# Scale and bias of the first feed-forward's activation: applied to the activation itself instead of behind the second matrix

## The chip, the core and the metric

The kernel runs on one core of one Trainium2 chip. The metric is the device time of one execution in microseconds (us). PE is TensorE (PEld its weight loads), DVE VectorE, ACT ScalarE, POOL GpSimd, and SP the engine that issues most DMAs. The core has on-chip memory (SBUF) and eight accumulator banks of 128 x 512 floats each (PSUM), into which PE writes.

## The reference: what is computed

Attention with a memory term over 4 batches, 8 heads, 576 positions and 64 features gives 2304 tokens of 512 values. Two feed-forwards follow:

```python
# first feed-forward: w_in 512 x 2048, w_out 2048 x 512, s and b one number each
h = x @ w_in
r = np.maximum(h, 0.0)
g = s * (r * r) + b
x = (g @ w_out).astype(np.float32)
# second feed-forward, same sizes
h = x @ w_in
P = a[0] + a[1] * h + a[2] * h2 + a[3] * h3        # h2 = h*h, h3 = h2*h
Q = 1.0 + np.abs(b[0]) * np.abs(h) + np.abs(b[1]) * h2
g = P / (Q + 1e-06)
return (g @ w_out).astype(np.float32)
```

Since s and b are single numbers, g @ w_out equals s * ((r * r) @ w_out) + b * (column sums of w_out). The kernel before uses the right-hand form; the changed kernel uses the left-hand one.

## The kernel before

The four weight matrices come as float64, the rest as float32. Each matrix product is taken as three products of a split pair (a high part in the reduced float32r format, and the rest), so an activation is always handed to PE as two tiles, high and low: `gh` and `gl`.

The program has these stages. Attention runs in 32 units (16 pairs of heads, low and high half of the positions), their tiles named q, k, vm, s (scores), p, pt/th (transposed probabilities), pf/fs (the memory term's input), av and xp (the output). While it runs, the weights of the first half of the first feed-forward are decoded from float64 (`decode`: one ACT and some five DVE or POOL instructions on 128 x 512; tiles dAi, dAo for the resident half, dB for the half that is stored to DRAM as `w1d`). Block A, nine pieces of 256 tokens, computes the first 1024 hidden features and stores a partial sum `x2p`; seven of the nine pieces are interleaved with attention. Block B, five pieces of 512, 512, 512, 384 and 384 tokens, does the other 1024 features, adds `x2p`, and stores `x2T`; meanwhile the second feed-forward's matrices are decoded (d2i, d2o). Block C, the same five pieces, is the second feed-forward.

In blocks A and B a step `up` multiplies by w_in into a bank `ha` or `hb`, `relu_square` (line 914) makes `gh` and `gl` of it, and a step `down` multiplies these by w_out. `interleave` puts up(f+1) between up(f) and down(f). `relu_square` before is: ACT relu to a tile `r`, ACT square of `r` to `gh`, DVE max(h,0)*r written back into the bank, DVE bank minus `gh` to `gl`. The square and the product need nothing of each other.

Scale and bias come behind block B (line 1027): one ACT instruction per output tile, with `sc1` as scale and the column `bcs` as bias. `bcs` is made from `wsum`, the sum over all decoded w_out tiles, which `decode` builds with one addition per w_out tile (`total`, line 430: 16 additions), and which four small matmuls with a vector of ones reduce (`colsum`, line 1251). The four parameter loads stand in `params` (line 1187), on SP's queue.

The order of instructions is not the code's order. `op` records each operation with the engines that may take it (`ways`, with an estimated cost), what it reads and writes, and a due time; `Plan.run` then simulates the five engines with these estimates, hands each operation to an engine, and emits it. Every engine then works through its list in order. An operation that disappears, or takes longer to become ready, thus moves others on all engines. POOL cannot read PSUM. PSUM banks are handed out in the same simulation and are free again when the last reader is done: the bank of `ha` or `hb` is held until `gl` is made.

Of the kernel before, what the change touches and what calls it, by code (L numbers as in the profile page):

```python
# [20 lines left out]
P = 128  # L21
# [4 lines left out]
def f32(ap):  # L26
    return ap.bitcast(F32)
# [221 lines left out]
def tile_kernel(ctx, tc, qk, vm, z, beta, w1i, w1o, s1, b1, w2i, w2o, a2, b2, out):  # L249
# [59 lines left out]
    nc.vector.tensor_tensor(both, ident[:, 0:64], ident[:, 64:128], ALU.add)  # L309
    wsum = cst.tile([P, DM], F32, name="wsum")  # L310
    nc.gpsimd.memset(wsum, 0.0)
    prm = cst.tile([P, 8], F32, name="prm")
    sc1, bi1 = prm[:, 0:1], prm[:, 1:2]
    a0, a1, a2_, a3 = (prm[:, 2 + i:3 + i] for i in range(4))
# [5 lines left out]
    nc.vector.memset(ones, 1.0)  # L320
    bcs = cst.tile([P, KC], F32, name="bcs")
    gate = cst.tile([P, H], F32, name="gate")
# [4 lines left out]
    omg = cst.tile([P, H], F32, name="omg")  # L327
    cst.tile([P, 40], F32, name="fill_c")
    buf("gate", None, obj=gate)
    buf("omg", None, obj=omg)  # L330
    buf("prm", None, obj=prm)
    buf("wsum", None, obj=wsum)
    buf("bcs", None, obj=bcs)
    for n in ("rec0", "rec1", "qd0", "qd1", "wsum"):
        plan.bufs[n].const = True
# [70 lines left out]

    def decode(src, nm, hi, lo, key, total=False):

# [31 lines left out]
    def w1_store(q, m, i):  # L440

        nm = f"{q}_{m}_{i}"
        parts = f"sh{nm}", f"sl{nm}"
        for n in parts:
            at_ring(n, n[:2], 2, [P, 512], F32R)
        decode(w1_source(1, q, m, i), f"dB{nm}", lambda: g(parts[0]), lambda: g(parts[1]), parts, m == 1)
        for x, n in enumerate(parts):
            load(lambda x=x: w1d[q, m, x, i], lambda n=n: f32(g(n)), P * 4 * 512, (n,), (("w1d", (q, m, x, i)),))
# [12 lines left out]
    def w1_half(k, pool):  # L461
# [12 lines left out]
        for q in range(HF // 4):  # L474
            for c in range(KC):
                sl = slice(q * 512, (q + 1) * 512)
                src = w1_source(k, q, 0, c)
                units.append(lambda c=c, q=q, sl=sl, src=src: decode(
                    src, f"d{nm}i{c}_{q}", lambda: inp("h", c, sl), lambda: inp("l", c, sl),
                    ((f"w1ih{nm}", (c, q)), (f"w1il{nm}", (c, q)))))  # L480
            for f in range(4 * q, 4 * q + 4):
                src = w1_source(k, q, 1, f % 4)
                units.append(lambda f=f, src=src: decode(
                    src, f"d{nm}o{f}", lambda: outp("h", f), lambda: outp("l", f),
                    ((f"w1oh{nm}", f), (f"w1ol{nm}", f)), True))
        return inp, outp, units
# [431 lines left out]
    def relu_square(HS, hs, w, nm):  # L918
# [9 lines left out]
        op(ways(w, -0.04), relu, (HS,), (R,))  # L928
        op(ways(w, 0.0), lambda e: e.activation(g(GH), g(R), AF.Square), (R,), (GH,))
        op(ways(w, None, 1.0), lambda e: e.scalar_tensor_tensor(hs(), hs(), 0.0, g(R), ALU.max, ALU.mult), (HS, R), (HS,))  # L930
        op(ways(w, None, 1.0), lambda e: e.tensor_tensor(g(GL), hs(), f32(g(GH)), ALU.subtract), (HS, GH), (GL,))
        return GH, GL
# [60 lines left out]
    def block_b(t0, w, at0, at1, inp, outp):  # L993
# [13 lines left out]
        def down(f):  # L1007
            GH, GL = parts[f]
            for c in range(KC):
# [11 lines left out]
                if f == HF - 1:  # L1021
# [171 lines left out]
    op(ways(1, 0.0), lambda e: e.activation(b1abs, prm[:, 7:8], AF.Abs), ("prm",), ("prm",))
# [68 lines left out]
    events.append((bB[0] - LOADS - 0.005, prior(bB[0] + 12.0, colsum)))
    for i, (t, w) in enumerate(wide):
# [85 lines left out]
```

## Time and profile before

| | us |
|---|---|
| median of 3 runs | 1061.24 |
| lowest, highest | 1059.4, 1061.42 |
| the profiled execution | 1060.15 |
| its span, first to last instruction | 1058.4 |
| PE busy in the span | 1016.3 (96%) |
| PEld, DVE | 868.7 (82%), 849.0 (80%) |
| ACT, POOL | 687.5 (65%), 414.9 (39%) |

The profiled execution lies between the lowest run and the median; 1.75 us of it lie outside the span. Busy shares are averages over the stages: attention with block A until about 406 us, the rest of block A to 456, block B to 660, block C to the end. A "wait" is idle time of an engine put down to what ended it; names after "<-" are what the instruction reads, or who released it. Buffer numbers are left out of the names, so `gla` stands for any `gl` of block A.

### The profile page before, as it was taken

The numbers are of one execution on the slowest core, as the hardware profiler recorded it, in microseconds if no ns is written. First come the engines' busy times: TensorE is split into PE (matmuls) and PEld (weight loads), VectorE is DVE, ScalarE is ACT, GpSimd is POOL, SyncE is SP. The second block draws the span as 40 slices with busy tenths as digits, with TensorE's granted clock in tenths as the row PEclk, the third lists the DMA queues.
The fourth block names the chain that finished last, engine by engine and source line by source line (L and its number), as shares of the span: only waits on it lengthen the run. The fifth ranks groups of instructions, "written<-read, shape, count | busy, mean of one in ns | idle before, by whom it ended". The sixth has DMA issues, their size and how long they took to land.

```text
span 1058.4 us, 17508 instructions
## 1 busy us (share of the span) xinstructions
PE 1016.3 (96%) x5980; PEld 868.7 (82%) x5980; DVE 849.0 (80%) x1511; ACT 687.5 (65%) x1449; POOL 414.9 (39%) x470
## 2 busy tenths in 40 slices
PE   5886999999999999999999999999999999999998
PEld 3565888878888789987778999888888888898997
DVE  5999987888779885479999543888888888887896
ACT  5866666676557653355554443877866877777895
POOL 2423221032002211012021002877777876876785
PEclk8998999999999999999999999999999999999999
DMA  6666566666656655986765332900200200010000
GB/s 196 203 191 189 150 194 207 170 201 192 192 158 187 181 176 174 365 254 206 254 204 194 102 99 65 325 1 1 78 1 0 70 1 1 23 41 1 30 1 31
DMA packets 88633, 140.42 MB, mean 133 GB/s; under 512 B 12408, under 2 KB 50400, under 8 KB 88544
## 3 DMA queue, kind: packets, MB, share of 16 engines
q1 hardware_dynamic: 83856, 130.52, 39.0%
q0 software_dynamic: 4224, 8.39, 2.5%
q8 instruction: 47, 0.77, 0.3%
q10 hardware_dynamic: 464, 0.40, 0.1%
q14 instruction: 42, 0.34, 0.1%
HBM read 103.56 MB, written 35.71 MB: 132 GB/s over the span
## 4 chain that ended last, share of the span: by engine, by line
PE 71%; DVE 13%; DMA 8%; ACT 3%; issue 2%; SPq 2%; POOL 0%; ACTq 0%; DVEq 0%; POOLq 0%
PE hc L913 19%; PE ac L1104 19%; PE ab L1017 7%; PE hb L913 7%; PE ha L913 6%; PE acc L978 6%; SPq L362 2%; PE av L857 2%; PE pt L525 2%; PE s L648 1%; DVE s L655 1%; DMA cb<-crow 1%; PE av L865 1%; DMA dAi_0r<-in_w1i 1%; PE su L682 1%
## 5 line engine op out<-in xcount | busy, mean ns | idle before, releaser
L1083 DVE RECIPROCAL qe<-qe 128x512 f32<-128x512 f32 (+2 forms) x82 | 242.6, 2959 | 49.4 <-POOL qe L378 49.4
L913 PE MATMUL hc<-xc_h,w2ih 128*128 128x512 f32 (+1 forms) x320 | 117.8, 368 | 0.0
L913 PE MATMUL hc<-xc_h,w2il 128*128 128x512 f32 (+1 forms) x320 | 117.8, 368 | 0.0
L913 PE MATMUL hc<-xc_l,w2ih 128*128 128x512 f32 (+1 forms) x320 | 117.7, 368 | 0.0
L378 POOL TENSOR_TENSOR qe<-qe,qb 128x512 f32<-128x512 f32 (+2 forms) x82 | 94.9, 1158 | 55.1 <-ACT qb L1068 54.2
L1104 PE MATMUL ac<-w2oh,ghc 128*128 128x512 f32 x288 | 112.6, 391 | 0.0
L1104 PE MATMUL ac<-w2ol,ghc 128*128 128x512 f32 x288 | 112.5, 391 | 0.0
L1104 PE MATMUL ac<-w2oh,glc 128*128 128x512 f32 x288 | 112.3, 390 | 0.0
L378 POOL TENSOR_TENSOR glc<-po,ghc 128x512 fp32r<-128x512 f32 (+2 forms) x82 | 95.0, 1158 | 23.2 <-ACT ghc L368 23.1
L378 POOL TENSOR_TENSOR pm<-pm,s 128x512 f32<-128x512 f32 (+2 forms) x82 | 95.3, 1162 | 17.1 <-ACT pm L1068 16.2
L525 PE MATMUL pt<-ident,p 128*128 128x128 f32 x320 | 62.0, 291 | 24.0 <-DVE xp L868 6.8
L1074 ACT ACTIVATE s<-hc 128x512 f32<-128x512 f32 (+2 forms) x82 | 44.6, 544 | 61.2 <-PE hc L913 58.3
L978 PE MATMUL acc<-gha,w1olA 128*128 128x256 f32 x288 | 83.7, 291 | 0.0
L978 PE MATMUL acc<-gla,w1ohA 128*128 128x256 f32 x288 | 81.5, 283 | 0.1
L978 PE MATMUL acc<-gha,w1ohA 128*128 128x256 f32 x288 | 81.3, 282 | 0.0
L666 ACT ACTIVATE p<-s,st 128x128 f32<-128x128 f32 (+3 forms) x128 | 66.5, 526 | 21.7 <-DVE st L655 20.4
L1068 ACT ACTIVATE pm<-hc,prm 128x512 f32<-128x512 f32 (+2 forms) x82 | 59.6, 726 | 22.4 <-DVE hc L1085 21.9
L525 PEld LDWEIGHTS pt<-ident,p 128*128 128x128 f32 x320 | 40.8, 147 | 38.9 <-ACT th L368 8.6
L913 PEld LDWEIGHTS hc<-xc_h,w2il 128*128 128x128 f32 x320 | 60.1, 188 | 9.1 <-DVE po L1087 0.4
L913 PEld LDWEIGHTS hc<-xc_l,w2ih 128*128 128x128 f32 x320 | 60.1, 188 | 8.6
L913 PEld LDWEIGHTS hc<-xc_h,w2ih 128*128 128x128 f32 x320 | 60.0, 188 | 7.4
L1068 ACT ACTIVATE qb<-s,cq,b1abs 128x512 f32<-128x512 f32 (+2 forms) x82 | 62.7, 764 | 2.1 <-POOL qe L378 2.1
(493 smaller groups left out, 2979.8 us busy)
## 6 DMA issues: line engine op xcount, KB each, us to landing
vm<-in_vm SPq DMA_DIRECT2D x16, 384.0 KB
k<-in_qk SPq DMA_DIRECT2D x32, 144.0 KB
x2p<-ev SPq DMA_DIRECT2D x18, 256.0 KB
out_y<-ob SPq DMA_DIRECT2D x18, 256.0 KB
qm<-in_vm SPq DMA_DIRECT2D x16, 256.0 KB
w1d<-sh SPq DMA_DIRECT2D x16, 256.0 KB
w1d<-sl SPq DMA_DIRECT2D x16, 256.0 KB
w2d<-sh SPq DMA_DIRECT2D x16, 256.0 KB
```

What stands on the lines that cost most here:

```text
L362: op({"SP": 0.1 + size / 350e3}, lambda e: e.dma_start(dst(), src()), r, w)
L378: op(ways(c, None, dve, pool), lambda e: e.tensor_tensor(dst(), x(), y(), alu), r, w, port=True)
L525: nc.tensor.transpose(dst[:, o:o + P], src, ident)
L666: e.activation(g(f"p{n}_{i}")[:, o:o + kb - ka], g(b)[:, o2:o2 + kb - ka], AF.Exp, scale=-1.0, bias=g(f"st{n}")[:, z_:z_ + 1], accum_out=g ...
L857: nc.tensor.matmul(g(AV)[64 * j:64 * j + 64, ra:rb], g(VS)[:, kb, j], g(TH)[:, o:o + rb - ra], start=x in firsts, stop=False, skip_group_c ...
L913: nc.tensor.matmul(hs(), m, y, start=c == 0 and k == 0, stop=c == KC - 1 and k == 2)
L978: nc.tensor.matmul(a, outp(y, f)[:, cs], g(z_)[:, us], start=f == 0 and k == 0 and c % 2 == 0, stop=f == HF - 1 and k == 2, skip_group_che ...
L1017: nc.tensor.matmul(g(ACC)[:, 0:w], outp(y, f)[:, cs], g(z_), start=f == 0 and k == 0, stop=f == HF - 1 and k == 2)
L1068: return lambda e: e.activation(g(dst)[:, ks], g(src)[:, ks], AF.Identity, scale=m, bias=b)
L1074: op(ways(c, -0.04), lambda e, ks=ks: e.activation(g(S2)[:, ks], g(HS)[:, ks], AF.Square), (HS,), part(S2))
L1083: op({"DVE": 0.07 + c * 0.00625}, lambda e, ks=ks: e.reciprocal(g(QE)[:, ks], g(QE)[:, ks]), part(QE), part(QE))
L1104: nc.tensor.matmul(g(ACC), g(x_)[:, ks], g(f"w2o{y}{i}")[:, o], start=f == 0 and q == 0, stop=f == NF - 1 and q == 2)
```

## The change

`wsum`, its memset, the 16 additions, the four small matmuls, `bcs` and the 20 ACT instructions behind block B are gone. `relu_square` now computes relu on ACT, then on DVE h * s * r into the bank, then `gh` = bank + b (ACT with the bias as a per-partition pointer, or DVE), then `gl` = (bank + b) - `gh` on DVE. So `gh` is made from the product, and no longer beside it. `s` and `b` have a tile of their own, `sb`, loaded early (due at 20 in the plan's time); the other two parameters stay with `params`.

```diff
-        if total:
-            pair_op(lambda: wsum, lambda: wsum, lambda: f32(g(F)), ALU.add, 512, (F, "wsum"), ("wsum",))
...
         op(ways(w, -0.04), relu, (HS,), (R,))
-        op(ways(w, 0.0), lambda e: e.activation(g(GH), g(R), AF.Square), (R,), (GH,))
-        op(ways(w, None, 1.0), lambda e: e.scalar_tensor_tensor(hs(), hs(), 0.0, g(R), ALU.max, ALU.mult), (HS, R), (HS,))
-        op(ways(w, None, 1.0), lambda e: e.tensor_tensor(g(GL), hs(), f32(g(GH)), ALU.subtract), (HS, GH), (GL,))
+        op(ways(w, None, 1.0), lambda e: e.scalar_tensor_tensor(hs(), hs(), sc1, g(R), ALU.mult, ALU.mult), (HS, R, "sb"), (HS,))
+
+        def high(e):
+            if e is nc.scalar:
+                e.activation(g(GH), hs(), AF.Identity, bias=bi1)
+            else:
+                e.tensor_scalar(g(GH), hs(), bi1, None, ALU.add)
+
+        op(ways(w, 0.15, 1.0), high, (HS, "sb"), (GH,))
+        op(ways(w, None, 1.0), lambda e: e.scalar_tensor_tensor(g(GL), hs(), bi1, f32(g(GH)), ALU.add, ALU.subtract),
+           (HS, GH, "sb"), (GL,))
...
-                    op(ways(w, 0.19), lambda e, PP=PP, c=c: e.activation(
-                        g(PP), g(PP), AF.Identity, scale=sc1, bias=bcs[:, c:c + 1]), (PP, "bcs"), (PP,))
...
+    def scale_bias(e):
+        for t, x in ((s1, sc1), (b1, bi1)):
+            e.dma_start(x, t.rearrange("(o h) -> o h", o=1).to_broadcast([P, 1]))
+
+    plan.at, plan.since = 20.0, 20.0
+    op({"SP": 1.0}, scale_bias, (), ("sb",))
...
-    def colsum():
-        bank("pw", UP)
-
-        def mm():
-            for c in range(KC):
-                nc.tensor.matmul(g("pw")[:, c:c + 1], wsum[:, c * P:(c + 1) * P], ones, start=True, stop=True)
```

What it does to the order, at three places. First DVE in block B's third piece, where `hb1024_3` is the bank of its fourth group of hidden features, `rb` the relu, and d2i tiles are of the decode. Before:

```order
L930 SCALAR_TENSOR_TENSOR hb1024_3_7635<-hb1024_3_7635,rb1024_3_7663 128x512
L931 TENSOR_TENSOR glb1024_3_7678<-hb1024_3_7635,ghb1024_3_7669 128x512
L419 TENSOR_SCALAR d2i3_2f_7684<-d2i3_2r_7616 128x512
L421 SCALAR_TENSOR_TENSOR d2i3_2f_7684<-d2i3_2r_7616,d2i3_2f_7684 128x512
L423 SCALAR_TENSOR_TENSOR d2i3_2f_7684<-d2i3_2r_7616,d2i3_2f_7684 128x512
L425 SCALAR_TENSOR_TENSOR d2i3_2f_7684<-d2i3_2m_7660,d2i3_2f_7684 128x512
L419 TENSOR_SCALAR d2i0_3f_7702<-d2i0_3r_7654 128x512
L421 SCALAR_TENSOR_TENSOR d2i0_3f_7702<-d2i0_3r_7654,d2i0_3f_7702 128x512
L930 SCALAR_TENSOR_TENSOR hb1024_4_7680<-hb1024_4_7680,rb1024_4_7709 128x512
L931 TENSOR_TENSOR glb1024_4_7721<-hb1024_4_7680,ghb1024_4_7716 128x512
```

After, the same stretch:

```order
L924 SCALAR_TENSOR_TENSOR hb1024_3_7610<-hb1024_3_7610,sb_106,rb1024_3_7635 128x512
L422 SCALAR_TENSOR_TENSOR d2i3_2f_7626<-d2i3_2m_7624,d2i3_2f_7626 128x512
L367 CAST w2ih1_6951<-d2i3_2f_7626 128x512
L933 SCALAR_TENSOR_TENSOR glb1024_3_7656<-hb1024_3_7610,sb_106,ghb1024_3_7650 128x512
L416 TENSOR_SCALAR d2i0_3f_7666<-d2i0_3r_7607 128x512
L418 SCALAR_TENSOR_TENSOR d2i0_3f_7666<-d2i0_3r_7607,d2i0_3f_7666 128x512
L420 SCALAR_TENSOR_TENSOR d2i0_3f_7666<-d2i0_3r_7607,d2i0_3f_7666 128x512
L422 SCALAR_TENSOR_TENSOR d2i0_3f_7666<-d2i0_3m_7641,d2i0_3f_7666 128x512
L924 SCALAR_TENSOR_TENSOR hb1024_4_7659<-hb1024_4_7659,sb_106,rb1024_4_7681 128x512
L375 TENSOR_TENSOR w2il0_6817<-d2i0_3f_7666,w2ih0_6811 128x512
L933 SCALAR_TENSOR_TENSOR glb1024_4_7700<-hb1024_4_7659,sb_106,ghb1024_4_7694 128x512
```

The two instructions of a chain stood next to each other; now two (for `hb1024_3`) or one decode instruction (for `hb1024_4`) stand between them.

ACT in the same stretch. Before:

```order
L418 ACTIVATE d2i3_2m_7660<-d2i3_2r_7616 128x512
L926 ACTIVATE rb1024_3_7663<-hb1024_3_7635 128x512
L929 ACTIVATE ghb1024_3_7669<-rb1024_3_7663 128x512
L418 ACTIVATE d2i0_3m_7690<-d2i0_3r_7654 128x512
L368 CAST w2ih1_6990<-d2i3_2f_7684 128x512
L926 ACTIVATE rb1024_4_7709<-hb1024_4_7680 128x512
L929 ACTIVATE ghb1024_4_7716<-rb1024_4_7709 128x512
```

After:

```order
L415 ACTIVATE d2i3_2m_7624<-d2i3_2r_7572 128x512
L921 ACTIVATE rb1024_3_7635<-hb1024_3_7610 128x512
L415 ACTIVATE d2i0_3m_7641<-d2i0_3r_7607 128x512
L928 ACTIVATE ghb1024_3_7650<-hb1024_3_7610,sb_106 128x512
L415 ACTIVATE d2i1_3m_7675<-d2i1_3r_7644 128x512
L921 ACTIVATE rb1024_4_7681<-hb1024_4_7659 128x512
L365 CAST w2ih0_6811<-d2i0_3f_7666 128x512
L928 ACTIVATE ghb1024_4_7694<-hb1024_4_7659,sb_106 128x512
```

`ghb` followed its relu directly; now a square or a cast of the decode stands between the two, on the same queue.

Second, DVE near the end of the start-up, up to `xp6`, the output of attention unit 6. Before (`wsum` is among the rows):

```order
L421 SCALAR_TENSOR_TENSOR dAi3_1f_1337<-dAi3_1r_1270,dAi3_1f_1337 128x512
L425 SCALAR_TENSOR_TENSOR dAo4f_1315<-dAo4m_1313,dAo4f_1315 128x512
L423 SCALAR_TENSOR_TENSOR dAi3_1f_1337<-dAi3_1r_1270,dAi3_1f_1337 128x512
L378 TENSOR_TENSOR wsum_105<-wsum_105,dAo4f_1315 128x512
L425 SCALAR_TENSOR_TENSOR dAi3_1f_1337<-dAi3_1m_1333,dAi3_1f_1337 128x512
L378 TENSOR_TENSOR w1olA_794<-dAo4f_1315,w1ohA_782 128x512
L591 TENSOR_REDUCE c2_7_1364<-tz7_1331 128x2x2
L868 TENSOR_TENSOR xp6_1368<-av6_1218,cb6_1317 128x192
```

After:

```order
L697 TENSOR_SCALAR rs7_1032<-rs7_1032 128x2x2
L375 TENSOR_TENSOR tz7_1334<-ph7_1268,zb3_684 128x256
L420 SCALAR_TENSOR_TENSOR dAi3_1f_1310<-dAi3_1r_1236,dAi3_1f_1310 128x512
L375 TENSOR_TENSOR w1olA_825<-dAo4f_1265,w1ohA_812 128x512
L422 SCALAR_TENSOR_TENSOR dAi3_1f_1310<-dAi3_1m_1314,dAi3_1f_1310 128x512
L700 RECIPROCAL rec1_97<-rs7_1032 128x2x2
L586 TENSOR_REDUCE c2_7_1364<-tz7_1334 128x2x2
L863 TENSOR_TENSOR xp6_1369<-av6_1221,cb6_1211 128x192
```

The addition to `wsum` is gone; a small instruction on `rs7`, which stood on POOL before, and the reciprocal `rec1` have come into the stretch, and `xp6` stands at almost the same place of DVE's list (row 243 for 241). Over the whole program the list of DVE grows from 1511 rows to 1517, that of ACT falls from 1285 to 1258 and that of POOL from 459 to 445: of the copies of transposed probabilities (`th`, 128 x 384) DVE has 23 where it had 15.

Third, SP's queue early in the program. After:

```order
L359 DMA dAi3_0r_405<-in_w1i 128x1024
L1186 DMA sb_106<-in_s1 128x1
L1186 DMA sb_106<-in_b1 128x1
L359 DMA zb2_419<-in_z 128x256
L359 DMA qm2_435<-in_vm 128x512
L359 DMA xTd0_117<-xp0_437 128x384
L359 DMA vm3_453<-in_vm 128x384
L359 DMA q6_470<-in_qk 64x192
```

The two loads of `sb` are new there; before, the load of zb2 followed that of dAi3_0r directly.

## Rows read from the trace of the kernel before

**Rows 1.** Busy time by stage: us, then each engine's busy us, granted clock, DMA share.

```profile
...
0.00:110.00 110.00, 84.21 (x532) 62.57 (x533) 92.83 (x268) 75.06 (x205) 33.05 (x73) 0.88 0.64 194
110.00:406.00 296.00, 285.73 (x2232) 243.59 (x2231) 238.92 (x708) 190.71 (x518) 53.93 (x110) 0.99 0.59 178
...
456.00:596.00 140.00, 137.94 (x622) 113.40 (x621) 127.74 (x203) 74.96 (x124) 21.18 (x16) 1.00 0.65 211
...
660.00:1058.40 398.40, 394.39 (x1821) 336.16 (x1819) 337.26 (x250) 303.78 (x527) 296.56 (x262) 1.00 0.13 41
...
```

**Rows 2.** Timeline, 91 to 105 us: start, length, engine, line, operation [idle, releaser].

```profile
...
95.78 0.68 DVE L378 TENSOR_TENSOR wsum<-wsum,dAo4f 128x512 f32<-128x512 f32 x1
...
97.92 0.34 DVE L868 TENSOR_TENSOR xp<-av,cb 128x192 f32<-128x192 f32 x1
...
98.32 0.48 PE L525 MATMUL pt<-ident,p 128*128 128x128 f32 x1 [6.81 <-DVE xp L868]
...
```

**Rows 3.** Waits of TensorE, 110 to 406 us: total us, times, longest.

```profile
...
PE pt L525 <- DVE gla L931: 2.1, 4, 1.4
...
```

**Rows 4.** Waits of the weight loads, 110 to 406 us.

```profile
...
PEld pt L525 <- DVE gla L931: 4.2, 5, 1.8
...
```

**Rows 5.** Instruction groups by shape: count, busy us, mean ns, idle before.

```profile
...
L930 DVE SCALAR_TENSOR_TENSOR ha<-ha,ra 128x512 f32<-128x512 f32 x36 | 25.0, 696 | 17.3 <-ACT ra L926 17.1
L931 DVE TENSOR_TENSOR gla<-ha,gha 128x512 fp32r<-128x512 f32 x36 | 24.7, 685 | 4.0 <-PE acc L978 2.2
...
L929 ACT ACTIVATE gha<-ra 128x512 fp32r<-128x512 f32 x36 | 22.8, 634 | 1.5 <-PE acc L978 1.0
...
L666 ACT ACTIVATE p<-s,st 128x512 f32<-128x512 f32 x32 | 21.8, 687 | 9.7 <-DVE st L655 9.2 <-DVE rec L705 0.6
...
L1027 ACT ACTIVATE pp<-pp,bcs,prm 128x512 f32<-128x512 f32 x12 | 8.9, 807 | 2.7 <-DVE pp L1025 2.7
...
```

**Rows 6.** The tile wsum: count, ns shortest/median/longest, first and last start.

```profile
...
L1256 PE MATMUL pw<-ones,wsum x8: 168/250/250, 467.6 to 468.3; 128*128 128x1 f32 x8
...
L378 POOL TENSOR_TENSOR wsum<-wsum,dB_1f x1: 1272/1272/1272, 220.1 to 220.1; 128x512 f32<-128x512 f32 x1
...
```

**Rows 7.** Timeline, 564.5 to 571 us, one chain of a 512-wide block.

```profile
...
564.43 0.39 PE L913 MATMUL hb<-xb_h,w1ihB 128*128 128x512 f32 x1
...
565.81 0.68 ACT L418 ACTIVATE d2i_2m<-d2i_2r 128x512 f32<-128x512 f32 x1 [2.00 <-DMA d2i_2r<-in_w2i]
...
566.39 0.58 ACT L926 ACTIVATE rb<-hb 128x512 f32<-128x512 f32 x1
...
567.61 0.69 DVE L930 SCALAR_TENSOR_TENSOR hb<-hb,rb 128x512 f32<-128x512 f32 x1
...
568.44 0.69 DVE L931 TENSOR_TENSOR glb<-hb,ghb 128x512 fp32r<-128x512 f32 x1
...
570.32 0.39 PE L1017 MATMUL ab<-glb,w1ohB 128*128 128x512 f32 x1
...
```

**Rows 8.** Timeline, 608.5 to 613.5 us, one chain of a 384-wide block.

```profile
...
610.32 0.56 DVE L931 TENSOR_TENSOR glb<-hb,ghb 128x384 fp32r<-128x384 f32 x1
...
613.23 0.33 PE L1017 MATMUL ab<-glb,w1ohB 128*128 128x384 f32 x1
...
```

**Rows 9.** Waits of TensorE, 456 to 596 us.

```profile
...
PE hb L913 <- DVE glb L931: 1.7, 2, 0.9
```

**Rows 10.** Waits of the weight loads, 456 to 596 us.

```profile
...
PEld hb L913 <- DVE glb L931: 2.6, 2, 1.3
PEld ab L1017 <- DVE glb L931: 2.0, 4, 0.6
```

**Rows 11.** Waits of ScalarE, 456 to 596 us.

```profile
...
ACT d2i_3m L418 <- DMA d2i_3r<-in_w2i: 5.5, 3, 2.1
...
```

**Rows 12.** DMA issues on SP's queue, 25 to 31 us.

```profile
...
26.95 0.38 SPq L362 DMA_DIRECT2D zb<-in_z  x1
27.97 0.33 SPq L362 DMA_DIRECT2D qm<-in_vm  x1
...
```

More of the change, by code (lines that the diff above doesn't have):

```diff
@@ L309, in tile_kernel @@
     nc.vector.tensor_tensor(both, ident[:, 0:64], ident[:, 64:128], ALU.add)
-    wsum = cst.tile([P, DM], F32, name="wsum")
-    nc.gpsimd.memset(wsum, 0.0)
     prm = cst.tile([P, 8], F32, name="prm")
-    sc1, bi1 = prm[:, 0:1], prm[:, 1:2]
+    sb = cst.tile([P, 2], F32, name="sb")
+    sc1, bi1 = sb[:, 0:1], sb[:, 1:2]
     a0, a1, a2_, a3 = (prm[:, 2 + i:3 + i] for i in range(4))
@@ L320, in tile_kernel @@
     nc.vector.memset(ones, 1.0)
-    bcs = cst.tile([P, KC], F32, name="bcs")
     gate = cst.tile([P, H], F32, name="gate")
@@ L327, in tile_kernel @@
     omg = cst.tile([P, H], F32, name="omg")
-    cst.tile([P, 40], F32, name="fill_c")
+    cst.tile([P, 42], F32, name="fill_c")
     buf("gate", None, obj=gate)
@@ L331, in tile_kernel @@
     buf("prm", None, obj=prm)
-    buf("wsum", None, obj=wsum)
-    buf("bcs", None, obj=bcs)
-    for n in ("rec0", "rec1", "qd0", "qd1", "wsum"):
+    buf("sb", None, obj=sb)
+    for n in ("rec0", "rec1", "qd0", "qd1"):
         plan.bufs[n].const = True
@@ L405, in ring, with decode @@
         plan.ring(name, role, roles[role], shape, dt)
-    def decode(src, nm, hi, lo, key, total=False):
+    def decode(src, nm, hi, lo, key):
         ring(f"{nm}r", "raw", [P, 512, 2], I32)
@@ L445, in w1_store @@
             at_ring(n, n[:2], 2, [P, 512], F32R)
-        decode(w1_source(1, q, m, i), f"dB{nm}", lambda: g(parts[0]), lambda: g(parts[1]), parts, m == 1)
+        decode(w1_source(1, q, m, i), f"dB{nm}", lambda: g(parts[0]), lambda: g(parts[1]), parts)
         for x, n in enumerate(parts):
@@ L484, in w1_half @@
                     src, f"d{nm}o{f}", lambda: outp("h", f), lambda: outp("l", f),
-                    ((f"w1oh{nm}", f), (f"w1ol{nm}", f)), True))
+                    ((f"w1oh{nm}", f), (f"w1ol{nm}", f))))
         return inp, outp, units
@@ L1182, in tile_kernel @@
     gates()
+    def scale_bias(e):
[3 more added lines that the diff above has]
+    op({"SP": 1.0}, scale_bias, (), ("sb",))
+    plan.since = 0.0
     for t, fn in sorted(events, key=lambda x: x[0]):
@@ L1187, in params @@
     def params(e):
-        for t, o, n in ((s1, 0, 1), (b1, 1, 1), (a2, 2, 4), (b2, 6, 2)):
+        for t, o, n in ((a2, 2, 4), (b2, 6, 2)):
             e.dma_start(prm[:, o:o + n], t.rearrange("(o h) -> o h", o=1).to_broadcast([P, n]))
     plan.at, plan.since = 60.0, 100.0
-    op({"SP": 2.0}, params, (), ("prm",))
+    op({"SP": 1.0}, params, (), ("prm",))
     op(ways(1, 0.0), lambda e: e.activation(b1abs, prm[:, 7:8], AF.Abs), ("prm",), ("prm",))
@@ L1249, in tile_kernel @@
         events.append((at0, lambda x=x: w1_fetch(*x)))
-    def colsum():
-        bank("pw", UP)
-        def mm():
-            for c in range(KC):
-                nc.tensor.matmul(g("pw")[:, c:c + 1], wsum[:, c * P:(c + 1) * P], ones, start=True, stop=True)
-        pe(100, mm, ("wsum",), ("pw",))
-        op(ways(4, None, 1.0), lambda e: e.tensor_scalar(bcs, g("pw")[:, 0:KC], bi1, None, ALU.mult), ("pw", "prm"), ("bcs",))
     events.append((bB[0] - LOADS - 0.005, lambda: roles.update(wider)))
-    events.append((bB[0] - LOADS - 0.005, prior(bB[0] + 12.0, colsum)))
     for i, (t, w) in enumerate(wide):
```

## The prediction

> **What bounds the kernel now.** I read the busy time by stage first, then the waits of TensorE in each stage, then one chain of block B as a timeline. PE is busy 394.39 of 398.40 us in block C, 137.94 of 140 us in the 512-wide part of block B, 285.73 of 296 us from 110 to 406 us, but only 84.21 of the first 110 us, at a granted clock of 0.88 [rows 1]. So from 110 us on the time is PE's work plus what PE waits, and the change can save there only what it takes from PE or from PE's waits. In the first 110 us DVE is the busiest engine (92.83 us), and PE's longest single wait, 6.81 us, ends when DVE gets to an `xp` [rows 2]. In the 512-wide part of block B DVE is busy 127.74 of 140 us, yet PE waits for `glb` only 1.7 us there [rows 1, 9]. The reader is to see that block B has two nearly full engines, with a chain between them that just fits.
>
> **The change part by part.** The sum is made against the profiled execution's 1060.15 us (its span of 1058.4 and 1.75 around it); it is 1.09 below the median of 1061.24, and what it gives is added to that median.
>
> *Small matmuls.* The four appear as 8 records (two passes each) that start from 467.6 to 468.3 us [rows 6], 0.1 us apart. They run on a full PE, so their 8 places go: -0.9.
>
> *ACT behind block B.* 20 instructions of 0.81 us or a little less [rows 5], four at the end of each piece, some 16 us of ACT. They lie beside PE's next `up`. What they delay is the first relu of the next piece; four such transitions, of which I count a little over 0.1 us each as reaching PE: -0.5 (bounds 0, and -3.2, four whole instructions).
>
> *Additions to wsum.* 14 on DVE at 0.68 [rows 2] and 2 on POOL at 1.27 [rows 6], 9.5 and 2.5 us. From 110 us on they lay beside a busy PE: nothing. Eight lie before about 115 us, where DVE is full: 5.4 us of its work. But the new order gives the place back: DVE's list is longer than before, the copies of `th` and other small work having come from ACT and POOL, and `xp6`, for which PE waited 6.81 us, stands at row 243 instead of 241. I take one addition that no longer stands ahead of it: -0.7. Bounds: -6.8, the whole wait, and +6.8, a wait of that size in another place, since the order of the first 110 us is new on all engines.
>
> *relu_square, durations.* DVE has the same two instructions per group: product 0.696, difference 0.685 [rows 5]; with a scalar as pointer I take the same. The square on ACT took 0.634 without a pointer; an ACT instruction of that width with a pointer bias and a PSUM source took 0.687 [rows 5]. 0.05 us more on an ACT that is busy 74.96 of 140 us [rows 1] costs nothing by itself.
>
> *relu_square, the chain.* Before, the square ran beside the product. Now `gh` lies between product and difference: 0.69 us and two hand-overs. From the end of the product to the start of the difference it was 0.14 us (567.61 + 0.69 to 568.44) [rows 7]; a hand-over between engines I bound by 0 and those 0.14 us, so each chain is 0.55 to 0.83 us longer. In the 384-wide pieces `glb` is ready at 610.88 and used at 613.23, a margin of 2.35 us [rows 8]: hidden. In the 512-wide pieces it is ready at 569.13 and used at 570.32, a margin of 1.19 [rows 7], since PE issues 26 matmuls from 564.43 to 570.32 and DVE and ACT are busy with the decode. Two things take more of the margin there than the 0.8. One or two decode instructions now stand between product and difference on DVE (0.4 to 0.7 us each), and on ACT a square of the decode, which waits for its load, may stand ahead of `gh`: before the relu such a wait was 2.00 us [rows 7], and three of one tile's waits came to 5.5 us [rows 11]. Behind the waiting `gh` on ACT are the next square and relu; DVE's difference waits for it, then the decode behind the difference, and PE for `glb`. Six times the margin was already zero in this stretch (two waits before `hb`, four before `ab`) [rows 10]. If these six pay 0.75 each, it is 4.5 us; where a piece of block B begins the new order puts nine matmuls of the next piece instead of six ahead of the last `down`, which gives back 0.7 on some. I take +3.0. Bounds: 0, if the margins take it all, and 14, half of the 24 chains at 1.2 (a PE that has waited gives the next chain the same time more).
>
> *relu_square, the banks.* The bank of `ha` is held until `gla` is made. From 110 to 406 us PE waited for `gla` before a transpose, 2.1 us by the matmuls and 4.2 in 5 waits by the weight loads that stand for the same stalls [rows 3, 4]. Five waits, 0.8 longer, are 4 us; the plan knows of the longer hold and puts other work there, so I take half: +2.0 (0 to 8, twice as many waits).
>
> *SP.* Two 128 x 1 loads come ahead of zb2 at 27 us. At 0.38 each, as zb's issue, they take 0.8 us of SP; behind zb2 SP stood idle from 27.33 to 27.97 [rows 12], which covers most of it: 0 (bounds 0 and +0.8). Later, two loads remain of four.
>
> Sum: -0.9 - 0.5 - 0.7 + 3.0 + 2.0 = +2.9. From 1060.15 this makes 1063.05, from the median 1064.1. I predict 1064 us.
>
> **The rivals.** *No change, 1061 us.* The chain's length is hidden: in both blocks PE has other work, since up(f+1) stands before down(f) and four banks let it run further ahead. Then +3.0 and +2.0 go, -0.9 and the rest of about -1.2 stay or are lost in the new order: 1059.5 to 1062, named 1061. For it: the 384-wide margin, and that PE hardly waits for `glb` now [rows 8, 9]. Against: six chains without margin [rows 10].
> The Trainium skill, Perfetto Trace Analysis, "Identifying the Most-Contended Engine", says that busy matmul time does not tell how near TensorE is to its limit, and that the share of busy weight loads does. By that rule PE has room in the 512-wide stretch (113.40 of 140 us, 81%), DVE at 91% is the bound [rows 1], and since DVE has as much to do as before, the time would not change: this rival. The trace speaks against it so far: PE issues every 0.227 us through the chain shown [rows 7], with no wait in it.
>
> *Faster, 1056 us.* The order of the first 110 us closes PE's wait of 6.81 us [rows 2]: in it PE has matmuls of block A between attention unit 6 and the transposes that need its bank, and DVE one addition fewer ahead of `xp6`. What PE saves there it keeps, since it is full from then on. With half of the chain's price: -6.8 - 0.9 - 0.5 + 2.5 = -5.7, hence 1055.5 to 1056. For it: DVE is full just there [rows 1], and ACT and POOL have lost some 19 us of work together. Against: DVE's own list is not shorter, and PE's work up to that point is the same; it decides the sign as soon as more than half of the wait goes.
>
> **How the numbers follow.** Forecast, slower: 0.43, with its own range of 1063.4 to 1069. No change: 0.27. Faster: 0.30. 0.2% (2.1 us) is about what a measurement of this kernel can tell from no change, and it separates the three cases: slower over 1063.4, faster under 1059.1. The range goes down to 1055, which takes in most of the faster case, and up to 1070, where the chain costs 9 us beside the other terms; some 0.1 lies on either side.
>
> **What would show it.** Right: `gl` in block B is ready 0.6 to 1.5 us later against the last matmul of its `up`, PE's waits for `glb` from 456 to 596 us grow from about 2 to about 5 us, its waits for `gla` from 110 to 406 us grow, block C takes the same 398 us, and the first 110 us end within 2 us of where they did. Wrong: PE waits no longer for `glb` or `gla` (then the margins were enough), or PE's busy time in the first 110 us differs by over 4 us either way (then the new order of the start-up decides, and the chain is a side matter).

## The result

| | median, us | lowest to highest | runs |
|---|---|---|---|
| before | 1059.69 | 1057.11 to 1061.42 | 6 |
| changed | 1067.22 | 1064.7 to 1070.05 | 6 |

The ratio is 1.0073, with a 95% interval of 1.005 to 1.0097: slower by 7.5 us, where +2.9 was forecast. The profiled execution took 1068.14 us, 1066.4 of it the span.

**The stages.** From here on a stage runs to the start of its last down matmul (`acc`, `ab`, `ac`). Units are the nine of block A; attention runs beside units 0 to 5. In us, from one profiled execution of each kernel; all but the first two are the runs told of below.

| kernel | to the end of unit 0 | units 1 to 3 | units 4, 5 | units 6 to 8 | block B | block C |
|---|---|---|---|---|---|---|
| before | 121.6 | 146.1 | 100.0 | 92.3 | 200.0 | 394.0 |
| changed | 119.1 | 148.8 | 106.7 | 89.6 | 199.1 | 398.7 |
| changed, tiles at 64 | 118.7 | 149.4 | 104.5 | 90.2 | 200.0 | 393.2 |
| changed, all at 32 | 118.6 | 147.7 | 104.3 | 90.0 | 197.1 | 393.2 |
| changed, left side +64 | 115.7 | 147.4 | 104.3 | 87.4 | 199.6 | 397.9 |
| changed, other distances | 119.9 | 148.9 | 104.3 | 89.3 | 200.5 | 398.5 |
| before, left side at 32 | 120.5 | 148.9 | 97.0 | 88.5 | 201.4 | 399.5 |
| removal alone | 117.5 | 147.2 | 107.4 | 89.6 | 199.7 | 393.9 |
| removal, order kept | 122.5 | 149.2 | 98.7 | 90.6 | 200.0 | 393.9 |
| chain alone | 118.7 | 154.4 | 96.9 | 92.4 | 199.1 | 394.1 |
| change, order kept | 125.7 | 149.7 | 102.1 | 89.1 | 217.7 | 394.0 |
| high part beside the product | 119.7 | 151.2 | 102.3 | 91.3 | 201.2 | 393.9 |
| changed, block A's weights +64 | 118.1 | 146.7 | 103.2 | 86.9 | 199.1 | 393.3 |
| order kept, all together | 123.3 | 145.8 | 99.2 | 87.3 | 200.9 | 394.0 |

Two stages lose: units 4 and 5 (+6.7), and block C (+4.7), in which no instruction and, behind its first few matmuls, no order was changed.

How far can one execution be trusted? Six kernels have the changed kernel's lists of instructions on every engine (the six rows that begin with "changed"); their units 4 and 5 take 103.2 to 106.7 us. Three have the lists of the kernel before (before, left side at 32, and removal with the order kept, which only lacks the removed rows): 97.0 to 100.0. So this loss comes with the order. In units 1 to 3 the two groups overlap (146.7 to 149.4 and 146.1 to 149.2), and nothing is to be read from them. The new order also moves work between stages: PE has 605 records up to the end of unit 0 where it had 617, 1099 in units 1 to 3 where it had 1110, and 771 in units 4 and 5 where it had 748. The 23 matmuls more are some 3 us of the +6.7 (an estimate, at 100.0/748 us each).

**The profile after.** Busy time by stage, as in [rows 1] (the last stretch begins 3.3 us later, as block B ends so much later):

```profile
0.00:110.00 110.00, 86.85 (x536) 62.48 (x537) 92.39 (x276) 75.37 (x207) 30.31 (x64) 0.91 0.66 195
110.00:406.00 296.00, 283.19 (x2196) 240.60 (x2196) 240.43 (x697) 187.31 (x506) 47.06 (x109) 0.98 0.59 177
456.00:596.00 140.00, 139.56 (x618) 113.16 (x617) 133.19 (x207) 66.39 (x111) 23.08 (x17) 1.00 0.66 213
663.30:1066.40 403.10, 399.08 (x1817) 335.57 (x1816) 337.46 (x250) 299.77 (x524) 295.93 (x262) 1.00 0.13 40
```

PE is busy 399.08 us in block C where it was 394.39 [rows 1], with no more matmuls: each takes longer. In the 512-wide stretch of B PE is fuller than before (139.56 against 137.94), so it waits less, not more. Its waits from 110 to 406 us (the lines with `gla` and `fl`) and from 456 to 596 us (`glb`), as total, times, longest; TensorE first:

```profile
PE pt L520 <- DVE gla L933: 5.6, 3, 3.0
...
PE pt L520 <- DVE fl L761: 1.3, 3, 0.8
...
PE hb L908 <- DVE glb L933: 0.4, 1, 0.4
```

and its weight loads:

```profile
PEld pt L520 <- DVE gla L933: 7.4, 6, 3.6
...
PEld hb L908 <- DVE glb L933: 0.9, 1, 0.9
PEld ab L1020 <- DVE glb L933: 0.7, 2, 0.4
```

Waits for `glb` shrank from 1.7 to 0.4 us, those for `gla` grew from 2.1 to 5.6 [rows 3, 4, 9, 10]. Neither is yet the price of the chain. PE also waits for `fl` (the low part of the memory term's input), and that fell as `gla` grew. Before:

```profile
PE pt L525 <- DVE fl L766: 4.5, 6, 1.4
```

And the `glb` waits did not fall because of the chain. With the same order and the tiles back at multiples of 64 (the first experiment) they are 2.8 us from 456 to 596 us. In the three runs of this order with the shorter matmuls of the kernel before they are 2.8, 0.8 and 2.1 us, in the three with longer ones 0.4 to 0.9. That fits a longer matmul that leaves DVE more time. The first experiment:

```profile
PE hb L908 <- DVE glb L933: 2.4, 1, 2.4
PE ab L1020 <- DVE glb L933: 0.4, 1, 0.4
```

The start-up's 6.8 us wait for `xp` [rows 2] is 0.3 us now; a 2.6 us wait for `fl` stands in its place (TensorE, 80 to 125 us):

```profile
PE ha L908 <- DVE fl L761: 2.6, 1, 2.6
...
PE pt L520 <- DVE xp L863: 0.3, 1, 0.3
```

The new relu_square, by shape over the whole execution (count, busy us, mean ns), beside [rows 5]:

```profile
L924 DVE SCALAR_TENSOR_TENSOR ha<-ha,sb,ra 128x512 f32<-128x512 f32 x36 | 27.2, 755 | 16.1 <-ACT ra L921 16.0
L933 DVE SCALAR_TENSOR_TENSOR gla<-ha,sb,gha 128x512 fp32r<-128x512 f32 x36 | 26.9, 746 | 10.1 <-ACT gha L928 8.8 <-PE acc L981 1.3
...
L928 ACT ACTIVATE gha<-ha,sb 128x512 fp32r<-128x512 f32 x35 | 24.1, 687 | 19.2 <-DVE ha L924 19.0
```

Product and difference take 60 ns more each (696 to 755, 685 to 746). ACT's 0.687 is the forecast value. An undisturbed chain shows the whole of it, relu, product, `gh` and difference. From the start of relu to the end of `gl` it takes 2.90 us:

```profile
442.77 0.60 ACT L921 ACTIVATE ra<-ha 128x512 f32<-128x512 f32 x1 [0.72 <-PE ha L908]
443.41 0.76 DVE L924 SCALAR_TENSOR_TENSOR ha<-ha,sb,ra 128x512 f32<-128x512 f32 x1 [0.57 <-ACT ra L921]
...
444.20 0.69 ACT L928 ACTIVATE gha<-ha,sb 128x512 fp32r<-128x512 f32 x1 [0.83 <-DVE ha L924]
...
444.92 0.75 DVE L933 SCALAR_TENSOR_TENSOR gla<-ha,sb,gha 128x512 fp32r<-128x512 f32 x1 [0.76 <-ACT gha L928]
```

An undisturbed chain before took 2.12 us, with 0.10 us between product and difference where there are 0.75 now:

```profile
439.64 0.60 ACT L926 ACTIVATE ra<-ha 128x512 f32<-128x512 f32 x1 [1.62 <-PE ha L913]
...
440.27 0.70 DVE L930 SCALAR_TENSOR_TENSOR ha<-ha,ra 128x512 f32<-128x512 f32 x1 [1.38 <-ACT ra L926]
...
441.07 0.69 DVE L931 TENSOR_TENSOR gla<-ha,gha 128x512 fp32r<-128x512 f32 x1
```

**Block C, matmul by matmul.** Four starts from the timeline of PE, before:

```profile
770.97 0.39 PE L913 MATMUL hc<-xc_h,w2il 128*128 128x512 f32 x1
771.20 0.39 PE L913 MATMUL hc<-xc_l,w2ih 128*128 128x512 f32 x1
771.43 0.39 PE L913 MATMUL hc<-xc_h,w2ih 128*128 128x512 f32 x1
771.65 0.39 PE L913 MATMUL hc<-xc_h,w2il 128*128 128x512 f32 x1
```

and after:

```profile
771.24 0.40 PE L908 MATMUL hc<-xc_h,w2il 128*128 128x512 f32 x1
771.47 0.40 PE L908 MATMUL hc<-xc_l,w2ih 128*128 128x512 f32 x1
771.71 0.40 PE L908 MATMUL hc<-xc_h,w2ih 128*128 128x512 f32 x1
771.94 0.40 PE L908 MATMUL hc<-xc_h,w2il 128*128 128x512 f32 x1
```

Three steps take 0.68 us before and 0.70 after; the reader is to look at such a step wherever a stage without waits grows. From the whole records: before, four in five of the 512-wide matmuls of block C start 226 or 227 ns apart; after, seven in ten are 230 to 236 ns apart.

What differs is where the tiles start. Each tile of the pool `cst` takes a multiple of 32 bytes of a partition. `wsum` (2048) and `bcs` go, `sb` comes, and the filler `fill_c` grows from 40 to 42 numbers, 160 to 168 bytes, which takes 192: all tiles of the left side (the weights, and some of the buffers of `xb`, `xc`, `ghb`, `ghc` and `glc`) move by 2016 bytes. By the addresses of the built programs every large tile began at a multiple of 64 bytes before; now those of the left side begin 32 bytes past one, those of the right side (`xa`, `gla`, `gha`, `glb` and the other buffers) still at one. Put against each matmul's own record, the starts of the moving operand (the tile that streams through PE) and of the weights loaded beside it decide: where both are on, or both off, a multiple of 64, the median step is 227 ns; where one is on and one off, 234. The weights in use and those loaded beside it start alike in nine of ten of these matmuls. Where only one of the two is unequal to the moving operand, the median is 231 ns (those loaded beside it, 87 matmuls) and 233 (those in use, 121), so the records do not tell which of the two counts.

### The profile page after: what moved, and what is told of

Same layout as the page of the kernel before. It is cut to its first block, busy times and chain, and to the rows that moved or that the text cites. A ratio compares the mean times of both kernels' runs of the same rounds, so it can differ in the third digit from the quotient of the medians.

```text
span 1066.4 us, 17417 instructions
## 1 busy us (share of the span) xinstructions
PE 1026.0 (96%) x5972; PEld 868.4 (81%) x5972; DVE 858.5 (81%) x1516; ACT 669.3 (63%) x1418; POOL 403.5 (38%) x458
## 4 chain that ended last, share of the span: by engine, by line
PE 72%; DVE 12%; DMA 9%; ACT 3%; issue 2%; SPq 2%; ACTq 0%; POOL 0%; DVEq 0%; POOLq 0%
PE ac L1105 19%; PE hc L908 19%; PE ab L1020 8%; PE hb L908 8%; PE ha L908 6%; PE acc L981 6%; PE av L852 2%; SPq L359 2%; PE pt L520 2%; DMA qm<-in_vm 1%; DVE s L650 1%; DMA cb<-crow 1%; ACT p L661 1%; PE s L643 1%; DMA dAi_1r<-in_w1i 1%
## 5 line engine op out<-in xcount | busy, mean ns | idle before, releaser
L908 PE MATMUL hc<-xc_h,w2ih 128*128 128x512 f32 (+1 forms) x320 | 118.7, 371 | 0.0
L1105 PEld LDWEIGHTS ac<-w2oh,ghc 128*128 128x128 f32 x288 | 54.0, 188 | 12.7
```

Source lines behind the costliest of these rows:

```text
L908: nc.tensor.matmul(hs(), m, y, start=c == 0 and k == 0, stop=c == KC - 1 and k == 2)
L1105: nc.tensor.matmul(g(ACC), g(x_)[:, ks], g(f"w2o{y}{i}")[:, o], start=f == 0 and q == 0, stop=f == NF - 1 and q == 2)
```

## The experiments

Ratios are to the kernel before, with 95% intervals.

**Tiles at multiples of 64, in the changed kernel.**

```diff
-    cst.tile([P, 42], F32, name="fill_c")
+    cst.tile([P, 40], F32, name="fill_c")
```

> The changed kernel, its filler tile 168 bytes wide made 160 again, so that every large tile starts at a multiple of 64 bytes of its partition, as in the kernel before (in the changed kernel all tiles of the left side start 32 bytes past one). The order of the instructions is the same. Theory of the starts (a matmul is slower when its moving operand and the weights loaded beside it start in different 32-byte halves of 64 bytes): the 512-wide matmuls go back from some 232 ns apart to 227, block C from 404 us to 398 to 399, block B is 2 to 3 us shorter; the 256-wide ones of block A go back from 118 to 119.5 ns, which costs 2.5 us; total 1059 to 1063, named 1061. Theory of the chain (the time lies in waits for glb and gla): nothing changes, 1066 to 1068, C stays at 404.

Measured: 1060.77 us, 1.0021 (1.0007 to 1.0035). The order is the changed kernel's on every engine. Block C is back at 393.2 us, the median 512-wide step at 227 ns in all blocks, the 256-wide one at 120. So two numbers in a filler are 0.5% of the 0.73%; the intervals of the two kernels do not meet.

**The kernel before, its left side moved by 32 bytes** (`fill_c` 48 numbers wide).

> The kernel before, its filler tile 32 bytes wider, so that all tiles of the left side start 32 bytes past a multiple of 64, as in the changed kernel; order the same. Theory of the starts: 512-wide matmuls 230 to 234 ns apart, block C 403 to 404 us, block B 2 to 3 us longer, block A's 256-wide ones 1.5 ns faster each (-2.5 us); total 1063 to 1068, named 1065. Theory of the chain: 1059 to 1061, no change.

Measured: 1064.31 us, 1.0048 (1.003 to 1.0065). Block C takes 399.5 us, with not one instruction changed. Mean lengths of two groups of 512-wide matmuls from 670 to 900 us; before:

```profile
L1104 PE MATMUL ac<-w2oh,ghc 128*128 128x512 f32 x172 | 66.9, 389 | 0.0
...
L913 PE MATMUL hc<-xc_h,w2ih 128*128 128x512 f32 x166 | 64.6, 389 | 0.0
```

before, moved by 32 bytes:

```profile
L1104 PE MATMUL ac<-w2oh,ghc 128*128 128x512 f32 x171 | 67.3, 394 | 0.0
...
L913 PE MATMUL hc<-xc_h,w2ih 128*128 128x512 f32 x161 | 63.4, 394 | 0.0
```

and the changed kernel with all tiles at 64:

```profile
L1105 PE MATMUL ac<-w2oh,ghc 128*128 128x512 f32 x170 | 66.2, 389 | 0.0
...
L908 PE MATMUL hc<-xc_h,w2ih 128*128 128x512 f32 x168 | 65.4, 389 | 0.0
```

**All tiles 32 bytes past a multiple of 64** (changed kernel, the right side's filler `fill_m` 112 instead of 120 numbers).

> The changed kernel with the tiles of the right side moved by 32 bytes too, so that all large tiles start 32 bytes past a multiple of 64. If it is the difference between the two starts that counts: 512-wide matmuls 227 to 228 ns apart, block C 398 to 400 us, total as with all at multiples of 64, 1059 to 1063. If each tile off a multiple of 64 costs by itself: 512-wide matmuls at 233 or more, block C 405 us or more, total 1067 to 1072. Theory of the chain: 1066 to 1068 with C at 404.

Measured: 1061.35 us, 1.0019 (1.0002 to 1.0036), median steps of 227, block C 393.2. No tile is "aligned", and nothing is lost: it is the difference between the two starts that counts.

**The left side 64 bytes on** (`fill_c` 56).

> The changed kernel, its filler tile 64 bytes wider than in the version with all tiles at multiples of 64: the left side's tiles are 64 bytes off a multiple of 128, the right side's on one. If the unit is 64 bytes: as with all at multiples of 64, 1059 to 1063, 512-wide matmuls 227 ns apart. If it is 128 bytes or more: as the changed kernel, 1066 to 1068, and 232 ns.

Measured: 1061.38 us, 1.0022 (1.0005 to 1.004): the time of the first theory with the pace of the second. 512-wide matmuls whose two starts differ by 64 take 233 ns, so the unit is not 64. But the 256-wide ones of block A take 114 instead of 120, and units 6 to 8 take 87.4 us instead of 90.2: the loss and a gain cancel. One group of block A from 410 to 450 us, before:

```profile
L978 PE MATMUL acc<-gha,w1ohA 128*128 128x256 f32 x51 | 14.4, 283 | 0.0
```

and with the left side 64 on:

```profile
L981 PE MATMUL acc<-gha,w1ohA 128*128 128x256 f32 x56 | 15.5, 276 | 0.0
```

**The removals alone** (`wsum`, its additions, `colsum` and the scaling taken out of the kernel before).

> The kernel before with the removals alone: no wsum, no additions to it, no small matmuls, no scaling behind block B; relu_square as it was (scale and bias of the first feed-forward are left out of the result). Tiles start at multiples of 64 bytes. By the prediction's terms -0.9 - 0.5 - 0.7 = -2.1 us against the kernel before: ratio 0.998. Rival (the order that the planner makes of the rest decides, and removals off the full engine give nothing): within 1 us of the kernel before or above it, with a difference between 0 and 310 us that has nothing to do with the removed work.

Measured: 1061.89 us, 1.0032 (1.0014 to 1.0049): less work, and slower. Units 4 and 5 take 107.4 us. A stall of it (start, length, idle before it):

```profile
273.14 0.68 ACT L413 ACTIVATE dB_0m<-dB_0r 128x512 f32<-128x512 f32 x1 [5.68 <-DMA dB_0r<-in_w1i]
273.14 0.43 DVE L414 TENSOR_SCALAR dB_0f<-dB_0r 128x512 int32<-128x512 int32 x1 [4.67 <-DMA dB_0r<-in_w1i]
...
274.91 1.32 PE L675 MATMUL su<-k,qd 128*128 128x288 f32 x3 [2.73 <-ACT th L363]
```

Both ACT and DVE stand still behind a decode whose load has not landed, and PE waits for the copy of `th` queued behind it. Here too 23 matmuls more than before lie in units 4 and 5 (771 records), and the granted clock is 0.97 over 268 to 375 us where it was 1.00.

**The removals, the order kept.** The planner still counts the operations; they issue nothing.

```diff
-            pair_op(lambda: wsum, lambda: wsum, lambda: f32(g(F)), ALU.add, 512, (F, "wsum"), ("wsum",))
+            op(ways(512, None, 1.0, 1.0), lambda e: None, (F, "wsum"), ("wsum",), port=True)
```

> The kernel before, from which exactly the removed instructions are left out (16 additions to wsum, the 4 small matmuls with their factor, 20 scalings behind block B), all others on all five engines in the order of the kernel before: the planner still counts them. Scale and bias are missing from the result. If it is the planner's new order that cost 0.3% in the run with the removals alone: here the removals give what the prediction's terms say, -2.1 us, ratio 0.997 to 0.999. If the removed work itself mattered the other way (fewer instructions in front of others, and the run is slower all the same): 1.002 to 1.004, as in that run.

Measured: 1057.27 us, 0.9982 (0.9964 to 1.0), -1.9 us. The same instructions in two orders lie 0.5% apart, and the intervals do not meet. The wait for `xp` is there as before (7.4 us, from 6.8 [rows 2]), though the addition to `wsum` ahead of it is gone.

**The chain alone** (the new relu_square and `sb` in the kernel before).

> The kernel before with the new relu_square alone (scale and bias come in a second time, and the sums and the scaling behind block B stay). Tiles start at multiples of 64 bytes. By the prediction's terms +3.0 in block B and +2.0 in block A: ratio 1.005, B's 512-wide stretch 3 us longer. Rival (hidden in B, since PE has its other matmuls there; only A pays): +1 to +3 us, all of it before 460 us, block B within 1 us of the kernel before. Rival (hidden everywhere): within 1 us.

Measured: 1061.65 us, 1.0022 (1.0008 to 1.0035). Block B is 0.9 us shorter than before; units 1 to 3 take 8.3 us more, units 4 and 5 3.1 less. The numbers are those of the first rival. That it is the chain which block A pays for is not shown, since the order is new here as well.

**The whole change, the order kept.** The removals issue nothing; ACT gets `gh` right behind its product:

```diff
+        def product(e):
+            e.scalar_tensor_tensor(hs(), hs(), sc1, g(R), ALU.mult, ALU.mult)
+            nc.scalar.activation(g(GH), hs(), AF.Identity, bias=bi1)
```

> The whole change in the order of the kernel before: the removed instructions left out, product and difference with scale and bias where they stood, and gh right behind its product on ACT; the two small loads go to ACT's queue; tiles at multiples of 64 bytes. If the longer chain costs what the prediction's terms say (+3.0 and +2.0 beside -2.1): ratio 1.002 to 1.004, PE waiting for gla and glb 5 us more. If the chain is hidden: as the removals alone in this order, 0.997 to 0.999.

Measured: 1084.82 us, 1.0246 (1.0224 to 1.0267), far over either expectation; 17.7 us of it in block B. The waits of ACT, 456 to 596 us:

```profile
ACT ghb L938 <- DVE hb L937: 39.8, 21, 4.6
...
```

and of TensorE there:

```profile
PE ab L1027 <- ACT ghb L938: 3.8, 4, 2.3
PE ab L1027 <- DVE glb L941: 3.4, 7, 1.4
PE hb L918 <- DVE glb L941: 3.4, 2, 2.8
```

Left where the square stood, `gh` blocks ACT for up to 4.6 us behind DVE's decode, and the next relus and squares with it. This is the mechanism that the prediction feared in block B, at six times its size. In the order that the planner makes with the longer chain in its estimates, block B does not pay it (199.1 us).

**The high part beside the product** (tiles at 64; ACT squares relu times the root of the scale, the order new).

> The changed kernel with all tiles at multiples of 64 bytes, and the high part made again from relu beside the product (ACT squares relu times the square root of the scale, which seven small DVE instructions make in the first 30 us); product and difference as in the changed kernel. If the longer chain is what the change itself costs (1.0021 with all tiles at 64): it goes, and the removals are left: ratio 0.997 to 0.999. If the cost is that of the order in block A, whatever the chain: 1.001 to 1.003.

Measured: 1065.21 us, 1.0052 (1.0035 to 1.0068). Without the longer chain it is slower still, and neither expectation holds: a third order, and units 1 to 3 and block B lose 5.1 and 1.3 us against the kernel before. With the order new again, the run does not separate the chain's price; it shows that taking the longer chain away gains nothing by itself.

**Other distances.** Block A's weights 224 to 384 bytes on, the right side 128.

> A look at the pace of the matmuls for other distances between the start of the weights that are loaded and that of the moving operand. The changed kernel with all tiles at 64, the right side's tiles moved by 128 bytes, and block A's four weight tiles used from 256, 320, 384 and 224 bytes further on: distances of 128, 192, 256 and 96 bytes (modulo 512) in block A, 0 and 128 in B and C. If the distance counts modulo 128: 119.5 ns at 128 and 256, and 227 ns in B and C. If modulo 512 or more: something else than at 0, in A 107 to 119 ns, in B and C 227 to 235 ns.

Measured: 1067.69 us in one run. Median steps in ns from these runs, by the start of the weights minus that of the moving operand, modulo 512 bytes; 480, 448 and 384 (the weights 32, 64 and 128 bytes behind) are counted as 32, 64 and 128 (in this run the distances alternate from matmul to matmul in block A):

| distance | 256 columns | 384 | 512 |
|---|---|---|---|
| 0 | 120 | 173 | 227 |
| 32 | 117 | 174 | 234 |
| 64 | 114 | 173 | 233 |
| 128 | 118 | 175 | 232 |
| 256 | 119 | not run | not run |

**Block A's weights 64 bytes on, all else at 64** (tiles at 64 as in the first experiment; the four weight tiles of block A are 128 numbers wider and used from number 16).

> The changed kernel with all tiles at multiples of 64 bytes, but the four weight tiles of block A used from 64 bytes further on (tiles 512 bytes wider, so that all others stay at the same place modulo 512). Theory of the starts: block A's 256-wide matmuls follow each other at 114 to 115 ns instead of 119.5, as with the whole left side 64 bytes on; B and C stay at 227; 1728 matmuls by 4.6 ns are 8 us, if PE bounds block A: ratio 0.995 to 0.996, 1053 to 1055. If block A is bound by its waits: a gain of 3 us or less, ratio 0.999 or above.

Measured: 1055.19 us, 0.996 (0.9946 to 0.9974), faster than both kernels. Its `acc` matmuls show the 276 ns again, B and C their 227. Units 6 to 8 take 86.9 us.

**All that the runs point to:** order kept, the root of the scale in relu, block A's weights 64 on.

> What the runs point to, with the reference's whole result: the removals in the order of the kernel before; the square root of the scale (seven small DVE instructions near the start) goes into relu on ACT, so that the square stays beside the product, and the bias into the difference; tiles at multiples of 64 bytes, block A's weights used from 64 bytes further on, B and C at 0 modulo 512. Parts: removals in this order 0.9982, block A's weights 0.996 against 1.0021, hence -1.9 and -6.4 us: ratio 0.992, 1051 to 1052 us. If the pointer operands of relu and product make the chain longer after all: 0.996 to 1.002. If the new pace of block A upsets the order that was laid out for the old one: 0.995 to 0.998.

Measured: 1056.88 us, 0.9985 (0.9967 to 1.0003), not the 0.992 of the sum. Units 6 to 8 have the gain (87.4 us), but the wait for `xp` is there again at 6.0 us, and one for `glb` of 2.1 in block B. Gains found in different orders did not add up. Relu, whose scale is now a pointer, takes 687 ns where it took 595, which the sum left out; before, and here:

```profile
L926 ACT ACTIVATE ra<-ha 128x512 f32<-128x512 f32 x36 | 21.4, 595 | 31.2 <-PE ha L913 28.2 <-issue 2.4 <-DVE ha L930 0.4
```

```profile
L941 ACT ACTIVATE ra<-ha,sb 128x512 f32<-128x512 f32 x36 | 24.7, 687 | 29.3 <-PE ha L928 23.7 <-DVE d2o1f L430 2.2 <-issue 2.0
```

## Why the prediction was right or wrong

The direction was right, and 1067 us lies in the range of 1055 to 1070, but that was luck in good part. The sum gave +2.9 us and +7.5 came. Of these, 5.5 us come from a term that the prediction held at nothing, the tiles that move. With the tiles in place 1.0021 is left, 2.2 us (0.7 to 3.7), close to the sum; but its largest term, +3.0 in block B, did not come, and stalls of the new order that stood in no term did.

*Block C unchanged.* This step failed. It was listed as a sign, "block C takes the same 398 us", and no term was made for tiles that move, though the edit removes tiles and takes `fill_c` from 40 to 42 numbers. Moving them costs 0.5% of the time, 5.5 us as the difference of 1.0073 and 1.0021. It agrees with the records: in block C 830 of the 512-wide matmuls have unequal starts, by 7 ns (234 - 227) 5.8 us, and C is 5.5 us longer than with the tiles at 64 (398.7 - 393.2). The 384 in block B would be 2.7 us, which the shorter waits for `glb` took in: B is 199.1 us for 200.0. In block A the steps are shorter, some 2.6 us in all (1728 by 1.5 ns, from 119.6 to 118.1 as means without the longest tenth).

*The removals.* Forecast -2.1, measured -1.9 with the order kept (-3.8 to 0). The sum fits; the three terms were not measured one by one, and the -0.7 for an addition ahead of `xp6` does not show, as that wait did not shrink (7.4 us). But the planner's new order takes 5.3 us (1.0032 less 0.9982) and turns the sign: the prediction gave the new order bounds in the first 110 us only, and none in units 4 and 5, where it costs most (107.4 us for 98.7, some 3 us of it moved work).

*The first 110 us.* Unit 0 ends 2.5 us earlier, though with 12 matmuls fewer ahead of its end. The faster rival's mechanism was real, the 6.8 us wait closed; but the gain was not kept, as the rival held it would be: in the new order units 4 and 5 lost more.

*Durations of relu_square.* ACT was right. For DVE "I take the same" was wrong by 60 ns an instruction, two per chain. The 634 to 687 ns on ACT hides two changes, as the last section shows.

*The chain.* Its length was right: 0.55 to 0.83 us forecast, 0.78 measured (2.90 less 2.12). Its place was not: +3.0 in block B became 0, as B takes 197.1 to 200.5 us in the six runs of the new order, for 200.0; that the price is real in another order, 17.7 us, is shown. For `gla` the waits grew by 3.5 us (TensorE) and 3.2 (weight loads) against +2.0 in bounds of 0 to 8, while those for `fl` fell by 3.2. The biggest one is a decode ahead of `gla`, as forecast for block B (changed kernel):

```profile
317.46 0.69 ACT L928 ACTIVATE gha<-ha,sb 128x512 fp32r<-128x512 f32 x1
...
320.41 0.43 DVE L416 TENSOR_SCALAR dB_3f<-dB_3r 128x512 int32<-128x512 int32 x1 [2.26 <-DMA dB_3r<-in_w1i]
320.76 0.74 DVE L933 SCALAR_TENSOR_TENSOR gla<-ha,sb,gha 128x512 fp32r<-128x512 f32 x1
...
321.56 0.88 PE L520 MATMUL pt<-ident,p 128*128 128x128 f32 x3 [3.02 <-DVE gla L933]
```

`gh` is ready at 318.15; the difference starts 2.6 us later, behind a decode on DVE that waits for its load, and PE stands for 3.02 us.

The wait costs more than its length. Behind it the granted clock falls from its upper level (1.00, 2.4 GHz) to its lower one (0.50, 1.2 GHz) until about 328 us, and PE gets through 19 matmuls in four us where it does 35 a little later, a loss of 1.8 us (an estimate, 16 of 35 matmuls):

```profile
324.00:328.00 4.00, 4.00 (x19) 3.35 (x20) 3.13 (x12) 3.57 (x13) 0.00 (x0) 0.50 0.59 180
332.00:336.00 4.00, 4.00 (x35) 3.41 (x34) 3.94 (x16) 3.57 (x13) 0.24 (x1) 1.00 0.51 144
```

All six kernels of this order have the fall, between 318 and 329 us; in units 4 and 5 of the three with the order before, the clock stays at 1.00. The prediction priced waits by their length alone.

*The rivals.* "No change" is not what the change gives with its tiles in place: 1.0021 (1.0007 to 1.0035) is nearer to the forecast's +2.9. But its mechanism, a hidden chain, holds in block B. The rule of the Trainium skill named with it (Perfetto Trace Analysis, "Identifying the Most-Contended Engine") would have had DVE as the bound of the 512-wide stretch; DVE went from 127.74 to 133.19 of 140 us there, and block B did not grow.

Open: which of the many moves of the new order makes each of the stalls in units 4 and 5, and how much of the 2.2 us with the tiles in place is the chain's and how much the order's. The runs show that units 4 and 5 are longer with this order, not that another would be free of stalls.

## What to carry to other kernels

When a change adds or takes away a tile, compare where all large tiles start before and after, and price a stage of bare matmuls by the step between starts: a few ns each are 0.5% here. With an order made by a planner, separate the work from the order (keep the operation in the plan and issue nothing): the removed work was worth -1.9 us and the reshuffle +5.3. Before comparing stages of two orders, count the work in each, and look at the granted clock behind each long wait. Where a matmul's weights start relative to its moving operand can be chosen, it pays to try: the best choice depends on the matmul's width.

## What the runs showed of the hardware

The step between matmuls depends on the distance between the start of the moving operand and that of the weights loaded beside it: a median of 227 ns at 0 (modulo 512 bytes) and 234 at 32 for 512 columns, but 120 at 0 and 114 at 64 for 256. The period was not found; 64 and 128 bytes are not it. Why wide matmuls lose and narrow ones gain was not settled, nor whether the weights in use or those loaded beside count.

The Trainium skill, SBUF — State Buffer, "Operand start alignment", says which starts are legal and that its runs timed nothing; its section "A bandwidth-pool intuition that's wrong (but worth ruling out)" gives weight loads an independent read port. The steps of 227 and 234 ns, from the same instructions at two places, speak against loads and moving reads that never meet; where they would meet is not shown.

A scale read through a pointer costs ACT 92 ns at 128x512: relu went from 595 to 687 in the last run, and the square from 634 to 727 in the run with the high part beside the product, each with nothing else about it changed:

```profile
L924 ACT ACTIVATE gha<-ra,sb 128x512 fp32r<-128x512 f32 x36 | 26.2, 727 | 1.9 <-PE acc L974 1.3
```

The 634 to 687 of the changed kernel shows less, as the function and the source changed too (from SBUF to PSUM; relu, from PSUM without a pointer, takes 595). On DVE the product took 755 ns with a pointer for 696 with a constant, and the difference 746 for 685; there the operations changed too (max to multiply, a subtraction to an addition and a subtraction), so the pointer's share was not separated.
